# A written order for the first two blocks of an attention and expert kernel

## The chip, the cores and the metric

The kernel runs on one core of one Trainium2 chip. The time is the device time of one execution in microseconds (us), and the time of a kernel is the median of several. One further execution is recorded by the hardware profiler. The engines have names of their own in the profile: PE is TensorE (PEld its weight loads), DVE is VectorE, ACT is ScalarE, POOL is GpSimd, and SP is SyncE, which here only issues transfers. All engines run their own queues in order and wait for one another by semaphores.

## What is computed

The reference is a linear attention, followed by two matrix products with a gate between them:

```python
q_s = exp(q - max(q, axis=-1));  q_s = q_s / (sum(q_s, axis=-1) + 1e-09)
k_s = exp(k - max(k, axis=2));   k_s = k_s / (sum(k_s, axis=2) + 1e-09)
kv = einsum('bhsd,bhse->bhde', k_s, v)
x  = einsum('bhsd,bhde->bhse', q_s, kv)        # 8 batches, 8 heads, 576 rows, 64 wide
h  = x.reshape(4608, 512) @ w_in               # 512 x 2048
g  = h * clip(h + 3.0, 0.0, 6.0) / 6.0
out = g @ w_out                                # 2048 x 512
```

The weights arrive as 64-bit floats. The kernel turns them into pairs of 32-bit numbers itself, a high part and a low part, and does each of the two large products in three passes: high by high, high by low, low by high.

## The kernel before

The 4608 rows are nine blocks of 512 (`j`). The inner width of 2048 is sixteen chunks of 128 (`f`). Each chunk has its own place of 1 MB in on-chip memory, first for the raw 64-bit weights (`raw`), then for their two parts (`w_0` to `w_15`).

**Decoding a chunk** (`decode`) is a fixed chain on two engines: `Abs` of the high words into a scratch tile `v` on ACT (L148), a clamp, a shift and the sign on DVE (L149, L151, L155), the low words scaled on ACT (L158), their addition on DVE (L159), and then the split: the high part is copied by ACT (L123, or L167), the low part is `v` minus that copy. For eleven chunks the subtraction is a DVE instruction (L124). For the five chunks 6, 8, 10, 12 and 14 (`BY_DMA`) ACT also writes `v` with scale -1, rounded as the high part is, into the place of the low part (L168), and a transfer issued by GpSimd adds `v` to it (L169, `w<-v`). There are three scratch tiles `v`; one comes free when its chunk's low part is done.

**Blocks 0 and 1** do the plain three passes. `gemm1(j, f)` is twelve matmuls of 512 columns into `ph`, then ACT's `Relu` (L841), DVE's product (L842), and the split of `g` into `g_hi` (ACT) and `g_lo` (DVE). `gemm2` is twelve matmuls into the four accumulators `po`, eight with `g_hi` and four with `g_lo`. While block 0 runs, the kernel also does the attention of block 1 for four pairs of heads, decodes all chunks, and begins to make other combinations of the weights (`fast_weights`, L463 to L485, written to `wf` in device memory). From block 2 on, two chunks at a time are done with seven products of half size (`fast_pair`), whose weights come back from `wf` into a ring of places (`fetch`).

**Attention of one pair of heads** in blocks 0 and 1: maximum over the transposed `k` (DVE `km`), exponential (ACT), transposes on PE (`pe`) and copies back (ACT), softmax over `q`, transposes (`tp`) and a copy, the product `pkv` of twenty small matmuls, three short DVE steps to `kv`, the product `px`, and its split into `x_hi` (ACT) and `x_lo` (DVE). In block 0 the subtraction and the product of the `q` softmax are on POOL.

**What sets the order.** In block 0 nothing is kept in the written order: the framework's scheduler sorts the instructions of each engine by its own timing of them, with a raised priority for a few (`soon`, `store`). With block 1, PE keeps the written order (`in_order`, L958), while DVE, ACT, POOL and SP are still sorted. From block 2 on, DVE, ACT and POOL too keep the written order (L984); there the work for the next block is spread over numbered places of the loop (`plan`, `tick`, 64 to a block, filled by `half`). SP issues nearly all loads and stores and is sorted by the scheduler throughout.

Of the kernel before, what the change touches and what calls it, by code (L numbers as in the profile page):

```python
# [18 lines left out]
P = 128  # L19
# [11 lines left out]
def attention_moe(  # L31
# [102 lines left out]
    BY_DMA = range(6, 15, 2)  # L134

    def decode(f):

        n = 2 * DM
        pairs = raws.pop(f).rearrange("p (n two) -> p n two", two=2)
        low, high = pairs[:, :, 0], pairs[:, :, 1]
        v = moe.tile([P, n], F32, name="v", bufs=3)
        m = v
        nc.scalar.activation(m, high.bitcast(F32), AF.Abs)  # L148
        nc.vector.tensor_scalar(m, m, W_MIN, W_MAX, op0=ALU.max, op1=ALU.min)  # L149
        m = m.bitcast(U32)  # L150
        nc.vector.tensor_scalar(  # L151
            m, m, 3, 0x3FFFFFFF, op0=ALU.logical_shift_left, op1=ALU.bitwise_and
        )
        vu = v.bitcast(U32)
        nc.vector.scalar_tensor_tensor(  # L155
            vu, high, 0xC0000000, m, op0=ALU.bitwise_and, op1=ALU.bitwise_or
        )
        nc.scalar.activation(low, low, AF.Copy, scale=2.0**-29)  # L158
        nc.vector.tensor_tensor(vu, vu, low, op=ALU.add)  # L159
        parts = place(f, F32R, f"w_{f}").rearrange("p (s i n) -> p s i n", s=2, i=2)  # L160
        vs = v.rearrange("p (s n) -> p s n", s=2)
        if f not in BY_DMA:
            split(parts[:, :, 0], parts[:, :, 1], vs)
        else:

            hi, lo = parts[:, :, 0], parts[:, :, 1]
            nc.scalar.copy(hi, vs)  # L167
            nc.scalar.mul(lo, vs, -1.0)  # L168
            nc.gpsimd.dma_start(lo.bitcast(F32), vs, accum_op=ALU.add)  # L169
        wi[f], wo[f] = parts[:, 0], parts[:, 1]  # L170
# [35 lines left out]
    def soon(j):  # L206
        return tc.high_priority() if j in (1,) else nullcontext()

    def kv_of(j, hp, ke, vt):

        pkv = ps_a.tile([P, TB], F32, name="pkv", tag="pa")
        for c in range(NCH):
            r = slice(0, P if c < NC4 or j >= FAST else TAIL)
            for h in range(2):
                hs = slice(h * D, (h + 1) * D)
                mm(pkv[hs, 0 : D + 1], ke[r, c, hs], vt[r, c, h, :], c == 0, c == NCH - 1)
        rk = att.tile([P, 1], F32, name="rk", bufs=2)
        kv = att.tile([P, P], F32, name="kv", bufs=5)
        with soon(j):
            nc.vector.tensor_scalar_add(rk, pkv[:, D : D + 1], EPS)  # L220
            nc.vector.reciprocal(rk, rk)
            nc.vector.scalar_tensor_tensor(
                kv.rearrange("p (h d) -> p h d", h=2),
                pkv[:, 0:D].rearrange("p (o d) -> p o d", o=1).broadcast_to([P, 2, D]),
                rk,
                mask.rearrange("p (h d) -> p h d", h=2),
                op0=ALU.mult,
                op1=ALU.mult,
            )
# [12 lines left out]
    def over(t):
        return t.rearrange("p (a o) -> p a o", o=1).broadcast_to([P, n8, D])

    def q_softmax(qt, lean, pool):

        qs = qt.rearrange("p c h d -> p (c h) d")
        qm = att.tile([P, n8], F32, name="qm", bufs=2)
        qr = att.tile([P, n8], F32, name="qr", bufs=2)
        if lean:  # L250
            nc.vector.tensor_reduce(qm, qs, axis=AX.X, op=ALU.max, negate=True)
            for i in range(n8):
                nc.scalar.activation(
                    qs[:, i],
                    qs[:, i],
                    AF.Exp,
                    bias=qm[:, i : i + 1],
                    accum_out=qr[:, i : i + 1],
                )
# [5 lines left out]
        nc.vector.tensor_scalar_add(qr, qr, EPS)
        nc.vector.reciprocal(qr, qr)
        pool.tensor_mul(qs, qs, over(qr))

    def k_softmax(j, km, ke, kt):

        nc.vector.tensor_reduce(km, kt, axis=AX.X, op=ALU.max, negate=True)
# [15 lines left out]

    def both_halves(stat, op):

        swap = att.tile([P, NG], F32, name="swap", bufs=2)  # L290
        for r in range(0, P, QD):
            o = r ^ QD
            nc.gpsimd.tensor_copy(swap[r : r + QD], stat[o : o + QD])
        nc.vector.tensor_tensor(stat, stat, swap, op=op)

    def q_softmax_t(qt):

        qs = qt.rearrange("p (g d) -> p g d", d=QD)
# [10 lines left out]
        nc.vector.tensor_mul(qs, qs, across(qr))
# [735 lines left out]
```

## Time and profile before

| | us |
|---|---|
| median of 3 runs | 874.55 (874.45 to 874.63) |
| profiled execution | 874.31 |
| its span, first to last instruction | 872.5 |
| PE busy in the span | 847.6 (97%) |
| DVE busy | 622.1 (71%) |
| ACT busy | 448.7 (51%) |
| POOL busy | 81.2 (9%) |
| mean granted PE clock | 0.992 |

The profile's rows give start and length in microseconds, the engine, the line of the kernel, what is written from what, the count, and in brackets how long the engine stood idle before and for whom. Engines overlap the end of an instruction with the start of the next, so the distance from start to start is what an instruction costs in a full queue, and it is a little less than the length. The tables by stretch give busy time of each engine, with counts in brackets, then the granted PE clock (1.00 is full speed), the busy share of the transfer engines and their rate.

### The profile page before, as it was taken

Reading aid. Unit: us, or ns where it says so; the run is one execution under the profiler, and the core shown is the slowest. Engines: PE = TensorE matmul, PEld = TensorE weight load, DVE = VectorE, ACT = ScalarE, POOL = GpSimd, SP = SyncE. Lnnn points to the kernel's source line nnn. Section 1 sums busy time; section 2 is a strip of 40 time slices with the busy share of each in tenths; the row PEclk is TensorE's granted clock in tenths of the full one; section 3 lists DMA queues with packets and bytes.
Section 4 is the critical chain, followed back from the end, with each engine's and each line's share of the span. In section 5 each row is a group of like instructions: output and inputs, shape, how many; then the busy total and the mean of one; then the engine's idle time right before and its main releaser. Section 6 shows DMA issues by size and latency. Waiting matters only on the chain.

```text
span 872.5 us, 15188 instructions
## 1 busy us (share of the span) xinstructions
PE 847.6 (97%) x5380; PEld 736.7 (84%) x5380; DVE 622.1 (71%) x1271; ACT 448.7 (51%) x907; POOL 81.2 (9%) x256
## 2 busy tenths in 40 slices
PE   4799999999999999999999999999999999999998
PEld 3577777788888998989899998999898998989996
DVE  7999997787467777777776767676767766664333
ACT  7999654444344545444544444445444545454333
POOL 5000121010101010101010101010101010100000
PEclk9899999999999999999999999999999999999999
DMA  9995454538387677767786778576865676557541
GB/s 370 413 389 142 111 165 133 167 101 301 103 282 239 194 240 247 242 196 247 230 260 185 244 210 270 180 238 207 274 202 167 188 220 191 172 167 220 178 135 48
DMA packets 98203, 184.67 MB, mean 212 GB/s; under 512 B 9808, under 2 KB 24144, under 8 KB 96080
## 3 DMA queue, kind: packets, MB, share of 16 engines
q1 hardware_dynamic: 96192, 180.03, 63.9%
q0 software_dynamic: 1360, 2.62, 1.8%
q10 hardware_dynamic: 576, 1.05, 0.3%
q8 instruction: 43, 0.70, 0.3%
q14 instruction: 32, 0.26, 0.1%
HBM read 156.93 MB, written 24.12 MB: 207 GB/s over the span
## 4 chain that ended last, share of the span: by engine, by line
PE 85%; DMA 2%; ACT 2%; DVE 1%; issue 0%; ACTq 0%
PE po L91 42%; PE ph L91 33%; PE pz L91 4%; PE px L91 3%; PE pkv L91 2%; DMA w<-v 1%; DMA wf<-w 1%; ACT w L123 0%; PE pm L97 0%; ACT v L148 0%; DVE g L584 0%; DVE w L124 0%; DVE ob L874 0%; ACT w L585 0%; ACT w L168 0%
## 5 line engine op out<-in xcount | busy, mean ns | idle before, releaser
L91 PE MATMUL po<-w,w 128*128 128x512 f32 x1008 | 262.2, 394 | 0.0
L91 PEld LDWEIGHTS po<-w,w 128*128 128x128 f32 x1008 | 176.5, 189 | 28.7
L91 PE MATMUL ph<-w,w 128*128 128x256 f32 x1008 | 147.3, 282 | 0.4 <-ACT second L559 0.4
L91 PEld LDWEIGHTS ph<-w,w 128*128 128x128 f32 x1008 | 139.4, 189 | 9.7 <-ACT second L559 0.8
L91 PE MATMUL ph<-x_lo,w 128*128 128x256 f32 (+1 forms) x800 | 146.4, 304 | 0.1
L91 PE MATMUL ph<-x_hi,w 128*128 128x256 f32 (+1 forms) x592 | 138.4, 338 | 1.4 <-DVE g L842 1.2
L91 PEld LDWEIGHTS ph<-x_lo,w 128*128 128x128 f32 x800 | 114.1, 190 | 12.2 <-issue 0.4
L91 PEld LDWEIGHTS ph<-x_hi,w 128*128 128x128 f32 x592 | 97.3, 191 | 20.4 <-DVE x_lo L124 1.8
L653 POOL COPY swap<-qm 32x16 f32<-32x16 f32 x192 | 48.5, 253 | 489.3 <-DVE qm L647 483.3
L91 PE MATMUL po<-w 128*128 128x512 f32 x336 | 88.2, 395 | 0.0
L582 ACT ACTIVATE g<-second,three 128x512 f32<-128x512 f32 x56 | 40.5, 724 | 68.9 <-DVE second L580 67.7
L91 PE MATMUL po<-w,g_hi 128*128 128x512 f32 x256 | 67.9, 402 | 0.4 <-ACT g_hi L123 0.4
L91 PEld LDWEIGHTS po<-w 128*128 128x128 f32 x336 | 58.7, 188 | 10.3 <-ACT w L585 0.5
L124 DVE TENSOR_TENSOR w<-g,w 128x512 fp32r<-128x512 f32 x56 | 38.8, 693 | 32.1 <-ACT w L123 31.7
L91 PEld LDWEIGHTS po<-w,g_hi 128*128 128x128 f32 x256 | 46.7, 188 | 11.3 <-ACT g_hi L123 0.5
L584 DVE SCALAR_TENSOR_TENSOR g<-g,second 128x512 f32<-128x512 f32 x56 | 38.7, 691 | 23.0 <-ACT g L582 23.0
L539 DVE SCALAR_TENSOR_TENSOR g<-g,ph 128x256 f32<-128x256 f32 x56 | 23.5, 420 | 44.3 <-ACT g L538 44.0
L585 ACT CAST w<-g 128x512 fp32r<-128x512 f32 x56 | 34.8, 621 | 31.9 <-DVE g L584 31.9
L538 ACT ACTIVATE g<-ph,three 128x256 f32<-128x256 f32 x56 | 26.3, 470 | 45.5 <-PE ph L91 45.4
L91 PE MATMUL pz<-x_hi,w 128*128 128x256 f32 x336 | 49.1, 282 | 0.0
L586 DVE TENSOR_TENSOR w<-g,w 128x512 fp32r<-128x512 f32 x56 | 38.8, 693 | 13.8 <-ACT w L585 12.0
L539 DVE SCALAR_TENSOR_TENSOR g<-g,first 128x256 f32<-128x256 f32 x56 | 23.6, 422 | 34.8 <-ACT g L538 34.8
(158 smaller groups left out, 1219.9 us busy)
## 6 DMA issues: line engine op xcount, KB each, us to landing
w<-wf SPq DMA_DIRECT2D x392, 256.0 KB, 3.0
raw<-in_w_dram SPq DMA_DIRECT2D x16, 1024.0 KB, 13.4
out_dram<-ob SPq DMA_DIRECT2D x36, 256.0 KB, 3.3
vt<-in_v_dram SPq DMA_DIRECT2D x28, 325.0 KB, 5.1
wf<-w SPq DMA_DIRECT2D x16, 512.0 KB, 4.4
kt<-in_kT_dram SPq DMA_DIRECT2D x28, 288.0 KB, 3.1
ke<-in_k_dram SPq DMA_DIRECT2D x24, 320.0 KB, 4.1
qt<-in_qf_dram SPq DMA_DIRECT2D x28, 256.0 KB, 3.5
```

The source lines that it names most:

```text
L91: nc.tensor.matmul(out, lhsT, rhs, start=start, stop=stop, skip_group_check=goes_on)
L124: engine.tensor_sub(lo, src, hi.bitcast(F32))
L538: nc.scalar.activation(r, h, AF.Relu, bias=three, scale=1.0)
L539: nc.vector.scalar_tensor_tensor(r, r, 6.0, h, op0=ALU.min, op1=ALU.mult)
L582: nc.scalar.activation(r, second, AF.Relu, bias=three, scale=1.0)
L584: nc.vector.scalar_tensor_tensor(r, r, 6.0, second, op0=ALU.min, op1=ALU.mult)
L585: rest.append(lambda: nc.scalar.copy(two[0], r))
L586: rest.append(lambda: nc.vector.tensor_sub(two[1], r, two[0].bitcast(F32)))
L653: nc.gpsimd.tensor_copy(swaps[hp][r : r + QD], qms[hp][o : o + QD])
```

## The change

All steps of block 0, of the attention of block 1, and of the decoding are cut into small functions, one or two instructions each, and one list of names (`STEPS`) says in which order they are written. The list holds for DVE, ACT, POOL, PE and, for its length, SP. A unit `a0` to `a3` is a pair of heads of block 0 (in the order 0, 2, 1, 3), `b0` to `b3` one of block 1, `w0` to `w15` a chunk's decoding, `g0` to `g15` a chunk's `gemm1` and, as `A` and `B`, the two halves of its `gemm2`. For block 1 DVE, ACT, POOL and PE keep a written order as well, given by `tick` as in later blocks; the attention of block 2 now goes through `half`, and all of `fast_weights` is placed there too, behind block 0. `BY_DMA` keeps only chunk 7. `x_factors`, with its four GpSimd subtractions, is gone.

```diff
-    BY_DMA = range(6, 15, 2)
+    BY_DMA = (7,)
     def decode(f):
...
-        if f not in BY_DMA:
-            split(parts[:, :, 0], parts[:, :, 1], vs)
-        else:
-            hi, lo = parts[:, :, 0], parts[:, :, 1]
-            nc.scalar.copy(hi, vs)
-            nc.scalar.mul(lo, vs, -1.0)
-            nc.gpsimd.dma_start(lo.bitcast(F32), vs, accum_op=ALU.add)
+        def hi():
+            nc.scalar.copy(parts()[0], st["v"].rearrange("p (s n) -> p s n", s=2))
+        def lo():
+            hi, lo = parts()
+            vs = st["v"].rearrange("p (s n) -> p s n", s=2)
+            if f not in BY_DMA:
+                nc.vector.tensor_sub(lo, vs, hi.bitcast(F32))
+            else:
+                nc.gpsimd.dma_start(lo.bitcast(F32), vs, accum_op=ALU.add)
+        def mul():
+            vs = st["v"].rearrange("p (s n) -> p s n", s=2)
+            nc.scalar.mul(parts()[1], vs, -1.0)
...
+    STEPS = """
+        a0.k_max b0.ld_kt a0.q_max a0.q_sub a0.k_exp a1.k_max a1.k_exp a1.k_flip a1.q_max
...
+        b0.kv2 g1.B b1.k_exp w4.hi w7.load w8.load w4.lo w5.sign b1.q_max w6.mag b0.kv3
...
+    """
+    def block0(u):
+        for step in STEPS.split():
+            unit, name = step.split(".")
+            u[unit][name]()
+    def at(j, n, *fns):
+        plan.setdefault((j, n), []).extend(fns)
+    def block1():
+        for p in range(NFC // 2 - 1):
+            d = fast_weights(p)
+            for n in (0, 1, 3, 4, 5, 7):
+                at(1, 8 * (p + 1) + n, lambda d=d: next(d, None))
+        d7 = fast_weights(NFC // 2 - 1)
+        for n in (0, 1, 3, 4, 5, 8):
+            at(2, n, lambda: next(d7, None))
+        for j in range(FAST, NB):
+            lead = {FAST: 3, FAST + 1: 6}.get(j, 0)
+            half(j, 0, 2, lead)
+            half(j, 1, 3, 32, 2 if j == FAST else 0)
+        fill()
+        for f in range(NFC):
+            g = gemm1(1, f)
+            tick(1, 4 * f)
+            tick(1, 4 * f + 1)
+            g.mms()
+            g.relu()
+            tick(1, 4 * f + 2)
+            g.times()
+            g.hi()
+            if f % 2 and f >= 11:
+                fetch(2 if f < 15 else 12 - len(come))
+            keep = f == NFC - 1
+            if not keep:
+                fill(6)
+            tick(1, 4 * f + 3)
+            gs = g.lo()
+            if not keep:
+                fill(6)
+            pend.append(work(1, [f], [gs]))
+    with tc.manual_schedule(engines=ORDERED | {mybir.EngineType.SP}):
+        block0(begin())
     with tc.manual_schedule(engines=ORDERED):
+        block1()
         for j in range(FAST, NB):
```

Three places show what moves. The first is DVE in block 0, around the last splits of `x` (`x_lo0`) that the first `gemm1` needs; `v` is the scratch tile of a chunk (before, `v_326` is chunk 1, `v_358` chunk 2, `v_414` chunk 3, `v_462` chunk 4; after, `v_281` chunk 1, `v_297` chunk 2). Before:

```order
L124 TENSOR_TENSOR x_lo0_311<-px_314,x_hi0_310 128x512
L159 ISA v_358<-raw2_118,v_358 128x2048
L221 RECIPROCAL rk_293<-rk_293 128x1
L149 TENSOR_SCALAR v_414<-v_414 128x1024
L222 SCALAR_TENSOR_TENSOR kv_294<-pkv_282,rk_293,mask_86 128x128
L124 TENSOR_TENSOR w_1_333<-v_326,w_1_333 128x2x512
L151 TENSOR_SCALAR v_414<-v_414 128x1024
L124 TENSOR_TENSOR x_lo0_311<-px_318,x_hi0_310 128x512
L124 TENSOR_TENSOR w_2_365<-v_358,w_2_365 128x2x512
L155 SCALAR_TENSOR_TENSOR v_414<-raw3_120,v_414 128x1024
L149 TENSOR_SCALAR v_462<-v_462 128x1024
L124 TENSOR_TENSOR x_lo0_311<-px_322,x_hi0_310 128x512
```

And the same place of DVE in the changed kernel:

```order
L386 TENSOR_TENSOR x_lo0_314<-px_326,x_hi0_313 128x512
L161 SCALAR_TENSOR_TENSOR v_281<-raw1_118,v_281 128x1024
L161 SCALAR_TENSOR_TENSOR v_297<-raw2_120,v_297 128x1024
L171 ISA v_281<-raw1_118,v_281 128x2048
L386 TENSOR_TENSOR x_lo0_314<-px_335,x_hi0_313 128x512
L386 TENSOR_TENSOR x_lo0_314<-px_342,x_hi0_313 128x512
L273 TENSOR_REDUCE km_366<-kt_130 128x1
L171 ISA v_297<-raw2_120,v_297 128x2048
L151 TENSOR_SCALAR v_364<-v_364 128x1024
L187 TENSOR_TENSOR w_1_369<-v_281,w_1_369 128x2x512
L155 TENSOR_SCALAR v_364<-v_364 128x1024
L187 TENSOR_TENSOR w_2_375<-v_297,w_2_375 128x2x512
```

The low parts of chunks 1 and 2 stood ahead of the last `x_lo0`; they now stand behind it.

The second place is PE, where the first `gemm2` of block 0 (`po`) comes (before, `w_305`, `w_365`, `w_421` are chunks 0, 2, 3). Before:

```order
L91 MATMUL ph<-x_lo_311,w_365 128x512
L91 MATMUL ph<-x_hi_310,w_365 128x512
L91 MATMUL po<-w_305,g_hi 128x512 x8
L91 MATMUL po<-w_305,g_lo 128x512 x4
L91 MATMUL ph<-x_hi_310,w_421 128x512
L91 MATMUL ph<-x_lo_311,w_421 128x512
```

In the changed kernel (`w_289`, `w_369`, `w_418`, `w_525` are chunks 0, 1, 3, 4):

```order
L89 MATMUL ph<-x_lo_314,w_418 128x512
L89 MATMUL ph<-x_hi_313,w_418 128x512
L89 MATMUL po<-w_289,g_hi 128x512 x8
L89 MATMUL po<-w_289,g_lo 128x512 x4
L89 MATMUL po<-w_369,g_hi 128x512 x8
L89 MATMUL po<-w_369,g_lo 128x512 x4
L89 MATMUL ph<-x_hi_313,w_525 128x512
```

The first `gemm2` stood behind the `gemm1` of three chunks; it now stands behind that of four, and two chunks' `gemm2` follow each other.

The third place is SP, behind the first six raw chunks. Before:

```order
L130 DMA raw6_336<-in_w_dram 128x2048
L325 DMA kt_368<-in_kT_dram 128x576
L330 DMA vt_371<-in_v_dram 128x650
L332 DMA qt_373<-in_q_dram 128x512
L130 DMA raw7_392<-in_w_dram 128x2048
L330 DMA vt_595<-in_v_dram 128x650
L332 DMA qt_597<-in_q_dram 128x512
L130 DMA raw14_802<-in_w_dram 128x2048
L130 DMA raw12_688<-in_w_dram 128x2048
```

In the changed kernel:

```order
L259 DMA kt_130<-in_kT_dram 128x576
L264 DMA vt_292<-in_v_dram 128x650
L268 DMA qt_299<-in_q_dram 128x512
L128 DMA raw6_362<-in_w_dram 128x2048
L429 DMA wf0_1375<-w_0_289 128x2x256 x2
L429 DMA wf0_1375<-w_1_369 128x2x256
L259 DMA kt_415<-in_kT_dram 128x576
L264 DMA vt_507<-in_v_dram 128x650
L268 DMA qt_509<-in_q_dram 128x512
L128 DMA raw7_527<-in_w_dram 128x2048
```

The load of chunk 7 now stands behind stores of chunks 0 and 1 and behind the second pair of heads of block 1 (`kt_415`), whose single buffer comes free with the first pair's transposes.

More of the change, by code (lines that the diff above doesn't have):

```diff
@@ new lines, in decode, with load, raw, mag @@
+        st = {}
+        def load():
+            load_w(f)
+        def raw(which):
+            return raws[f].rearrange("p (n two) -> p n two", two=2)[:, :, which]
+        def mag():
+            st["v"] = v = moe.tile([P, n], F32, name="v", bufs=3)
+            nc.scalar.activation(v, raw(1).bitcast(F32), AF.Abs)
+        def clamp():
+            v = st["v"]
+            nc.vector.tensor_scalar(v, v, W_MIN, W_MAX, op0=ALU.max, op1=ALU.min)
+        def shift():
+            vu = st["v"].bitcast(U32)
+            nc.vector.tensor_scalar(
+                vu, vu, 3, 0x3FFFFFFF, op0=ALU.logical_shift_left, op1=ALU.bitwise_and
+            )
@@ L172, in attention_moe @@
+        return dict(
+            load=load, mag=mag, clamp=clamp, shift=shift, sign=sign, lows=lows, plus=plus, hi=hi, mul=mul, lo=lo
+        )
     FAST = 2
@@ L840, in gemm1, with mms @@
-        g = moe.tile([P, TB], F32, name="g", bufs=2)
-        nc.scalar.activation(g, ph, AF.Relu, bias=three, scale=1.0)
-        nc.vector.scalar_tensor_tensor(g, g, 6.0, ph, op0=ALU.min, op1=ALU.mult)
-        g_hi = moe.tile([P, TB], F32R, name="g_hi", bufs=3)
-        g_lo = moe.tile([P, TB], F32R, name="g_lo", bufs=3)
-        split(g_hi, g_lo, g)
-        return g_hi, g_lo
+        st = {}
+        def mms():
+            x_hi, x_lo = x_tiles[j]
+            st["ph"] = ph = ps_h.tile([P, TB], F32, name="ph", tag="ph")
+            for cc in range(NCC):
+                first, last = cc == 0, cc == NCC - 1
+                w_hi, w_lo = (wi[f][:, i, cc * P : (cc + 1) * P] for i in (0, 1))
+                mm(ph, w_hi, x_hi[:, cc, :], first, False)
+                mm(ph, w_hi, x_lo[:, cc, :], False, False)
+                mm(ph, w_lo, x_hi[:, cc, :], False, last)
@@ L848, in gemm2, with lo, A, B @@
+        def lo():
+            g_hi, g_lo = st["gs"]
+            nc.vector.tensor_sub(g_lo, st["g"], g_hi.bitcast(F32))
+            return st["gs"]
+        def A():
+            st["work"] = work(j, [f], [st["gs"]])
+            B()
+        def B():
+            for got in [next(st["work"]) for _ in range(6)]:
+                run(got)
+        return SimpleNamespace(mms=mms, relu=relu, times=times, hi=hi, lo=lo, A=A, B=B)
     def gemm2(f, g_hi, g_lo, po):
@@ L977, in attention_moe, with begin @@
[L977 to L983 removed]
+    AHEAD = 6
+    HEADS = (0, 2, 1, 3)
+    def begin():
+        nc.scalar.activation(three, three, AF.Exp)
+        nc.gpsimd.memset(three, 3.0)
+        u = {}
+        for n, hp in enumerate(HEADS):
+            load_first(hp)
+            u[f"a{n}"] = early(0, hp)
+            u[f"a{n}"]["load"]()
+            u[f"b{n}"] = early(1, hp)
+            if n == 1:
+                load_w(0)
+            if n > 1:
+                load_first_v(HEADS[n - 2])
+        for hp in HEADS[2:]:
+            load_first_v(hp)
+        for f in range(NFC):
+            if 0 < f < AHEAD:
+                load_w(f)
+            u[f"w{f}"] = decode(f)
+            u[f"g{f}"] = vars(gemm1(0, f))
+        return u
```

502 lines of the change are left out of this document (209 added, 293 removed).

## The prediction

> **What bounds the kernel now.** I read the busy times by stretch first, cut where PE's work changes: at the first large matmul (33.45 us), at a point late in the first quarter of block 0, and at the first matmul of block 1 (143.4 us).
>
> ```profile
> 0.00:33.45 33.45, 16.81 (x124) 10.80 (x124) 28.16 (x52) 27.37 (x40) 11.32 (x19) 0.90 0.96 385
> 33.45:59.08 25.63, 23.90 (x116) 18.83 (x117) 25.63 (x39) 24.17 (x57) 0.00 (x0) 0.93 1.02 415
> 59.08:143.40 84.32, 81.94 (x402) 64.32 (x401) 77.77 (x128) 58.38 (x109) 12.60 (x29) 0.98 0.55 149
> 143.40:234.50 91.10, 91.10 (x467) 73.28 (x466) 66.43 (x134) 40.56 (x75) 8.79 (x16) 1.00 0.51 170
> ```
>
> The columns are length, then PE, PEld, DVE, ACT, POOL, then PE's clock. From 143.4 us PE is busy for 91.10 of 91.10 us. Ahead of it PE misses 16.64, 1.73 and 2.38 us, and its clock is at 0.90, 0.93 and 0.98, while DVE is busy nearly throughout. So the kernel is bound by PE's work, plus what PE loses in the first 143 us. PE's matmuls are the same before and after; a change of the early order is worth what it takes from these losses. PE's own time line names them:
>
> ```profile
> 27.26 1.13 PE L91 MATMUL px<-kq,kv 128*128 128x512 f32 x2 [1.48 <-DVE x_lo L124]
> 31.21 2.04 PE L91 MATMUL px<-kq,kv 128*128 128x512 f32 x2 [2.82 <-DVE kv L222]
> 33.45 0.79 PE L91 MATMUL ph<-x_hi,w 128*128 128x512 f32 x1 [0.20 <-DVE x_lo L124]
> ...
> 47.45 1.19 PE L91 MATMUL po<-w,g_lo 128*128 128x512 f32 x4 [1.33 <-DVE g_lo L124]
> ...
> 53.15 2.13 PE L91 MATMUL po<-w,g_hi 128*128 128x512 f32 x8 [0.39 <-ACT g_hi L123]
> ...
> 82.16 0.43 PE L91 MATMUL px<-qT,kv 128*128 128x64 f32 x2 [0.69 <-ACT qT L366]
> 83.81 0.50 PE L91 MATMUL ph<-x_hi,w 128*128 128x512 f32 x1 [1.22 <-DVE g L842]
> ...
> 87.92 0.73 PE L91 MATMUL ph<-x_hi,w 128*128 128x512 f32 x2
> ...
> 108.50 0.43 PE L91 MATMUL px<-qT,kv 128*128 128x64 f32 x2 [0.47 <-ACT qT L366]
> ...
> 143.41 0.40 PE L91 MATMUL ph<-x_hi,w 128*128 128x512 f32 x1
> ```
>
> Behind 33.45 us PE stands 1.33 + 0.39 + 0.69 + 1.22 + 0.47 = 4.10 us. A stop can also halve the clock, though the one of 1.33 us at 47 us did not:
>
> ```profile
> 30.00:32.00 2.00, 0.79 (x1) 0.50 (x2) 2.00 (x5) 1.90 (x3) 0.00 (x0) 0.53 1.08 426
> ...
> 46.00:48.00 2.00, 0.67 (x3) 0.48 (x3) 2.00 (x5) 2.00 (x12) 0.00 (x0) 1.00 0.99 418
> ...
> 82.00:84.00 2.00, 0.62 (x3) 0.49 (x4) 2.00 (x4) 1.95 (x4) 0.00 (x0) 1.00 0.96 274
> 84.00:86.00 2.00, 2.00 (x7) 1.58 (x7) 2.00 (x4) 1.48 (x3) 0.00 (x0) 0.68 0.41 146
> 86.00:88.00 2.00, 2.00 (x6) 1.52 (x6) 2.00 (x5) 2.00 (x5) 0.10 (x1) 0.50 0.01 4
> ```
>
> ```profile
> 111.79 2.79 PE ph L91 x12
> ```
>
> Twelve matmuls at full clock take 2.80 us, 0.233 each (the chain of waits, above). From 83.81 to 87.92 us eleven go by in 4.11 us instead of 2.57: 1.55 us more. The first eight of `gemm1` at 33.45 us lose as much, since PE had stood for 2.82 us.
>
> **The change, term by term.** *First term: the start of `gemm1`.* It waits for the third split of `x`, which sits in DVE's queue.
>
> ```profile
> 4.39 0.75 DVE L271 TENSOR_REDUCE km<-kq 128x1 f32<-128x576 f32 x1 [4.39 <-DMA kq<-in_kT_dram]
> ...
> 18.57 3.02 POOL L267 TENSOR_TENSOR kq<-kq,qr 128x512 f32<-128x512 f32 x2 [3.86 <-DVE qr L265]
> ...
> 18.91 1.79 DVE L124 TENSOR_TENSOR w<-v,w 128x1024 fp32r<-128x1024 f32 x1
> ...
> 32.72 0.68 DVE L124 TENSOR_TENSOR x_lo<-px,x_hi 128x512 fp32r<-128x512 f32 x1
> ```
>
> What the steps in it cost:
>
> ```profile
> L155 DVE SCALAR_TENSOR_TENSOR v<-raw,v 128x1024 uint32<-128x1024 uint32 x16 | 20.1, 1257 | 0.1
> L159 DVE CUSTOM_DVE_ANT_0 v<-raw,v 128x2048 uint16<-128x2048 uint16 x16 | 19.5, 1218 | 0.1
> L124 DVE TENSOR_TENSOR w<-v,w 128x1024 fp32r<-128x1024 f32 x11 | 13.9, 1266 | 1.1 <-ACT w L123 1.0
> L149 DVE TENSOR_SCALAR v<-v 128x1024 f32<-128x1024 f32 x16 | 11.4, 713 | 1.0 <-ACT v L148 1.0
> L151 DVE TENSOR_SCALAR v<-v 128x1024 uint32<-128x1024 uint32 x16 | 11.1, 696 | 0.0
> L124 DVE TENSOR_TENSOR g_lo<-g,g_hi 128x512 fp32r<-128x512 f32 x16 | 10.9, 684 | 0.0
> ```
>
> ```profile
> 69.01 0.68 DVE L124 TENSOR_TENSOR g_lo<-g,g_hi 128x512 fp32r<-128x512 f32 x1
> 69.61 0.68 DVE L842 SCALAR_TENSOR_TENSOR g<-g,ph 128x512 f32<-128x512 f32 x1
> 70.21 1.22 DVE L159 CUSTOM_DVE_ANT_0 v<-raw,v 128x2048 uint16<-128x2048 uint16 x1
> 71.35 0.74 DVE L271 TENSOR_REDUCE km<-kt 128x1 f32<-128x576 f32 x1
> ```
>
> From start to start a 512-wide step costs 0.60 us and a 1024-wide one with two sources 1.14; clamp and shift (L149, L151) have the 512-wide step's length and cost 0.60. In the new order one clamp, one shift, one addition and one subtraction fewer stand ahead of that third split: 2 x 0.60 + 2 x 1.14 = 3.48 us. This prefix ran slower than its sum before (about 25.4 us of such costs between the first `km` at 4.39 us and 33.40 us, less 0.8 us of waiting: a factor 1.11; the subtraction at 18.91 us took 1.79 us for 1.27 while POOL worked), so I take 3.48 x 1.11 = 3.9 us: `gemm1` starts at 29.5 us. Bounds: 2 us if the rest stretches more, 5.2 if POOL's share of the stretch falls as well. That PE still starts at half clock is left in: it stands between the last `px` and the split as it does now.
>
> *Second term: the stops behind it.* The first `gemm2` now stands behind four `gemm1`s, which gives `g_lo` of chunk 0 time. By the running sum over DVE's new order, the last split of `x` ends 0.60 behind the third, at 30.1 us; chunk 1's low part has 0.66 + 1.14 + 0.60 + 1.14 ahead of its end (33.6 us), chunk 2's 0.60 + 1.14 more (35.4), chunk 3's 2 x 1.14 + 4 x 0.60 + 1.14 more (41.2), chunk 4's 7.9 more (49.1), chunk 5's 9.1 more (58.2); `g_lo` of chunk 0 is out at 41.2 + 0.60 + 1.14 + 0.60 = 43.5. PE needs 2.80 + 1.55 us for the first `gemm1`, then 2.80 per twelve matmuls, about 0.95 per `pkv`, 0.5 per set of transposes and 1.0 per `px`: it comes to chunks 1 to 5 at 34.4, 37.2, 40.9, 49.3 and 59.2 us, and to `g_lo` of chunk 0 at 45.6. So the margins are thin for chunks 3 and 4 and there is no stop of a microsecond. Behind that, each chunk costs DVE 4.62 + 1.20 us and a sixteenth of its attention, PE 5.6 and the same; DVE is the slower one per chunk, but its steps stand up to two chunks ahead.
>
> *What the four transfers cost and what replaces them.*
>
> ```profile
> w<-v POOLq DMA_DIRECT2D x5, 512.0 KB, 5.1
> ```
>
> ```profile
> ACT v L148 <- DMA w<-v: 7.0, 2, 4.9
> ```
>
> ```profile
> L168 ACT ACTIVATE w<-v 128x1024 fp32r<-128x1024 f32 x5 | 5.3, 1067 | 0.0
> ```
>
> Each transfer lands 5.1 us after its issue and keeps one of three scratch tiles until then; ACT waited 7.0 us for two of them. Four go, with four ACT copies (4.3 us) and four issues on POOL. DVE gets four subtractions, 4 x 1.14 = 4.6 us. DVE's whole share of block 0 is then 15 x 4.62 + 3.48 for decoding, 16 x 1.20 for the gate and eight heads at about 3.15, 117 us; from 4.39 us, with 0.8 us of waiting and 2.8 us of early stretch, the last `g_lo` is out at 125 us and its `gemm2` at 128. That lies ahead of PE's own end below, so the added work is hidden behind PE; if it were not, it would cost its 4.6 us.
>
> So the stops behind 33.45 us, 4.10 us, and the slow clock at 84 us, 1.55, go. I put 0.7 us for new ones, the thin margins. Bounds: none, and 5.
>
> *Third term: block 1.* It now holds all attention of block 2 and all `fast_weights`. DVE has 66.4 of 91.1 us there; the `q` softmax of three pairs and four additions that ran ahead of it come on top:
>
> ```profile
> L463 DVE TENSOR_TENSOR m<-w 128x512 f32<-128x512 f32 x4 | 2.5, 676 | 0.0
> ...
> L309 DVE TENSOR_TENSOR qt<-qt,qr 128x512 f32<-128x512 f32 x3 | 2.1, 692 | 0.1
> ```
>
> Four steps like L309 for each of three pairs are 8.3 us, the additions 2.5, small ones about 1: some 12 us, 78 of 91, 0.86. Each matmul group's `g` has the 5.6 us of another group to be ready. I take 0; bounds: -0.4 (a small stop near block 2 goes) and, as a rival, 11.
>
> The sum goes against the profiled execution, 874.31 us: 874.31 - 3.9 - 4.10 - 1.55 + 0.7 = 865.5. The median of the runs is 0.24 us above that execution, so 865.7 us. Block 1 then starts at 143.4 - 8.85 = 134.6 us. A second count agrees: at 59.1 us PE has done 24 more matmuls than now and one `px`, 6.4 us; with 0.69 + 1.22 + 1.55 + 0.47 saved later that is 10.3 us, less 1.4 for handing over between engines that the running sum leaves out.
>
> The stop at 82 us halves the clock after 1.22 us without a large matmul. [...]
>
> **The rivals.** *PE keeps its clock over the gap ahead of `gemm1` (0.05).* Then the first eight matmuls cost 1.55 us less: 864.0 to 864.2. For it: 1.00 was granted behind the stop of 1.33 us. Against: the gap will be nearer to that of 2.82 us, which cost the clock. [...]
>
> *The thin margins break (0.17).* SP's queue has the load of chunk 7 behind a store that waits for chunk 1's low part, and ACT's copies of the low words stand behind loads. If chunks 3, 4, 5 and 7 each come 1 us late, PE stands 4 us, and once or twice drops its clock (1.55 us each): 865.7 + 4 + 2 = 871.7. For it: the same engines are full (24.17 and 25.63 of 25.63 us). Against: the loads run at 415 GB/s in that stretch, and a chunk of 1 MB takes 2.5 us.
>
> *Block 1 starves, slower than before (0.13).* One mechanism: DVE at 0.86 in a fixed order waits inside its queue for POOL's swaps, PE's transposes or a load, and `g_lo` behind it comes late for each of sixteen `gemm2`s. At 0.56 us per chunk it eats the 8.85 us; at 0.8 us, with one drop of the clock, it costs 16 x 0.8 + 1.55 = 14.3: 880. For it: in a written order nothing can be pulled ahead of such a wait. Against: the same written places run in later blocks with PE full.
>
> *It doesn't do what it says (0.05):* the engines meet at the same times, because attention's chain and not the queue sets `gemm1`; only the later stops go partly: about 872.5 to 874.
>
> **How the numbers follow.** Forecast 0.60, the kept clock 0.05, the thin margins 0.17, block 1 0.13, no effect 0.05. The likeliest gives 865.7 us. Its own range is 862.2 (start at 28.2, no new stop, the half clock gone) to 869. It holds some 0.6 with the kept clock; with the thin margins up to 872 the whole range is 862.2 to 872, and what is left out is the starved block 1 and no effect. A measurement tells 0.2%, 1.75 us, from no change: faster is below 872.8. The forecast, the kept clock and most of the thin margins (0.15) are below: 0.80; same, the rest of them and no effect, 0.07; slower, the starved block 1, 0.13.
>
> **What would show it.** The first matmul of `gemm1` at 29 to 30 us; the first of block 1 near 134.6; no wait of ACT for `w<-v`; no stop of PE over 1 us between 30 and 130 us, and a clock of 1.00 there after the start; DVE's last decoding subtraction near 122 us; PE full in block 1 and at the change to block 2. The forecast is wrong if `gemm1` starts after 32 us, if PE waits for `g_lo` or `x_lo` in block 1, or if a load of a chunk ends PE's wait.

## The result, and the profile after

The changed kernel takes **867.04 us** (865.12 to 867.68), the kernel before 874.53 in the same runs: a ratio of **0.991**, 95% interval 0.9897 to 0.9923. The profiled execution took 866.55 us, 7.76 less than the one before. First the busy times by stretch (columns as before), cut where PE's work changes now, and two short stretches around the first `gemm1`:

```profile
0.00:32.02 32.02, 15.12 (x124) 10.08 (x124) 24.59 (x48) 23.19 (x36) 10.69 (x19) 1.00 0.96 381
32.02:135.51 103.49, 103.48 (x516) 82.00 (x517) 96.51 (x141) 80.72 (x161) 1.33 (x1) 0.98 0.59 203
135.51:226.00 90.49, 90.49 (x467) 73.31 (x466) 76.75 (x159) 40.05 (x71) 9.97 (x32) 1.00 0.53 169
226.00:250.00 24.00, 23.66 (x148) 20.98 (x148) 18.42 (x38) 11.38 (x23) 1.09 (x4) 1.00 0.86 288
...
32.00:34.00 2.00, 1.98 (x7) 1.64 (x8) 2.00 (x3) 1.48 (x2) 0.00 (x0) 0.81 0.22 78
34.00:36.00 2.00, 2.00 (x6) 1.41 (x5) 2.00 (x3) 1.60 (x2) 0.00 (x0) 0.50 0.00 0
```

From the first `gemm1` at 32.02 us to block 1 at 135.51 PE is busy for 103.48 of 103.49 us, and block 1 is full; at the change to block 2 it stops once, for 0.34 us. The 4.10 us of stops are gone, and so is the slow clock at 84 us (1.00 was granted from 82 to 88 us). One half clock is left, behind the gap of 2.81 us ahead of `gemm1`. PE's own time line shows that gap and the start of block 1:

```profile
32.02 0.50 PE L89 MATMUL ph<-x_hi,w 128*128 128x512 f32 x1 [2.81 <-DVE x_lo L386]
...
36.95 0.47 PE L89 MATMUL ph<-x_hi,w 128*128 128x512 f32 x1
...
135.51 0.39 PE L89 MATMUL ph<-x_hi,w 128*128 128x512 f32 x1
```

(The row at 36.95 us is the second `gemm1`.) Block 1 starts 143.41 - 135.51 = 7.90 us sooner. Of this the earlier `gemm1` is 33.45 - 32.02 = **1.43 us**, the stops 4.10, the clock at 84 us 1.55; 0.82 I cannot assign.

The start is the surprise, so here is the beginning of ACT's and DVE's time lines, first after the change (a row with q behind the engine's name issues transfers; L225 is the load of `q`):

```profile
0.75 1.28 ACT L910 ACT_TABLE_LOAD   x1 [0.75 <-PEq L1073]
1.17 0.88 ACTq L225 DMA_DIRECT2D kq<-in_q_dram  x2
...
8.54 0.69 DVE L283 TENSOR_REDUCE qm<-kq 128x8 f32<-128x512 f32 x1 [2.27 <-DMA kq<-in_q_dram]
```

and before (L198):

```profile
0.75 0.41 ACTq L198 DMA_DIRECT2D kq<-in_q_dram  x1
1.19 1.28 ACT L880 ACT_TABLE_LOAD   x1 [1.19 <-PEq L1035]
1.25 1.35 ACTq L198 DMA_DIRECT2D kq<-in_q_dram  x3
...
6.31 0.68 DVE L261 TENSOR_REDUCE qm<-kq 128x8 f32<-128x512 f32 x1
```

The new `begin` writes ACT's table load ahead of all loads, and in a written order it stays there. So the first `q` load is issued at 1.17 instead of 0.75 us, and the second row maximum, the fourth step in DVE's queue, runs at 8.54 instead of 6.31 us, with DVE idle for 2.27 us before it.

### The profile page after: what moved, and what is told of

The parts are those of the page before. It is cut to its first block, busy times and chain, and to the rows that moved or that the text cites. A ratio compares the mean times of both kernels' runs of the same rounds, so it can differ in the third digit from the quotient of the medians.

```text
span 864.5 us, 15152 instructions
## 1 busy us (share of the span) xinstructions
PE 843.4 (98%) x5380; PEld 736.5 (85%) x5380; DVE 625.2 (72%) x1275; ACT 443.3 (51%) x897; POOL 70.7 (8%) x244
## 3 DMA queue, kind: packets, MB, share of 16 engines
q10 hardware_dynamic: 576, 1.05, 0.3%
## 4 chain that ended last, share of the span: by engine, by line
PE 95%; DVE 2%; DMA 1%; ACT 1%; issue 0%; POOL 0%; ACTq 0%; POOLq 0%
PE po L89 46%; PE ph L89 39%; PE pz L89 5%; PE px L89 3%; PE pkv L89 3%; DMA kq<-in_q_dram 1%; DVE v L161 0%; PE tp L95 0%; PE pm L95 0%; PE pe L95 0%; DVE x_lo L386 0%; DVE w L187 0%; DVE v L151 0%; DVE v L171 0%; DVE qr L308 0%
## 5 line engine op out<-in xcount | busy, mean ns | idle before, releaser
L620 POOL COPY swap<-qm 32x16 f32<-32x16 f32 x224 | 58.7, 262 | 627.9 <-DVE qm L614 593.9
```

What stands on the lines that cost most here:

```text
L620: nc.gpsimd.tensor_copy(swaps[hp][r : r + QD], qms[hp][o : o + QD])
```

## The experiments

Each is the changed kernel with one edit, except where said. Ratios are to the kernel before in the same runs, where it took 874.07 to 874.58 us.

### The q loads first

```diff
-        nc.scalar.activation(three, three, AF.Exp)
-        nc.gpsimd.memset(three, 3.0)
         u = {}
         for n, hp in enumerate(HEADS):
             load_first(hp)
...
         for hp in HEADS[2:]:
             load_first_v(hp)
+        nc.scalar.activation(three, three, AF.Exp)
+        nc.gpsimd.memset(three, 3.0)
```

> The changed kernel, but the four loads of q are issued by ACT ahead of its exponential table load (and the one-element exponential that asks for it), as in the kernel before. Theory Q, gemm1 starts late because the second q load lands late: DVE's idle 2.27 us at 8.54 us shrinks to under 0.8 (it was 0.8 in the kernel before), all of DVE's queue moves up by 1.5 us or so, gemm1 starts at 30.3 to 30.7 us instead of 32.02, nothing new stops behind it since DVE's later low parts move up as well, and the time is 867.0 - 1.5 = 865.5 us (865.0 to 866.2). Rival S, the start is set by the steps themselves stretched beside GpSimd and by the handing over between engines: the idle goes, but reappears in front of a later step, gemm1 still starts at 31.6 to 32.1 us, and the time is 866.6 to 867.4.

**864.96 us** (864.53 to 865.33), ratio 0.9896 (0.9882 to 0.9909). Its time lines of ACT, DVE and PE:

```profile
0.76 1.85 ACTq L225 DMA_DIRECT2D kq<-in_q_dram  x4
...
6.49 0.68 DVE L283 TENSOR_REDUCE qm<-kq 128x8 f32<-128x512 f32 x1
...
29.96 0.49 PE L89 MATMUL ph<-x_hi,w 128*128 128x512 f32 x1 [2.82 <-DVE x_lo L386]
```

and the stretch behind the start:

```profile
30.00:59.08 29.08, 29.08 (x138) 22.95 (x139) 29.08 (x41) 25.54 (x59) 0.00 (x0) 0.94 0.80 300
```

The second maximum comes at 6.49 us without a wait, all of DVE's queue moves up, `gemm1` starts 2.06 us sooner than in the changed kernel, and PE is full behind it. Theory Q, with a little more gained than it said. Since the intervals of the two kernels touched, both ran again side by side:

> The changed kernel, unchanged, beside the next one on one chip, since the two were so far timed apart (867.04 and 864.96 us with overlapping intervals). Theory Q (the late second q load): DVE's idle in front of the second q maximum is 2 to 3.5 us in the profile and the median 866.5 to 867.7. Rival R (the two differ by the chip and the day alone): the median is within 1 us of the next kernel's.

> The changed kernel with the four q loads ahead of ACT's table load, a second time, beside the changed kernel. Theory Q: gemm1 starts near 30 us, 864.5 to 865.7, 1.5 to 2.5 us below the changed kernel with an interval that excludes none. Rival R: within 1 us of it.

The changed kernel took 866.96 us (865.50 to 867.71), with the `q` loads first 864.64 (864.47 to 864.85): 2.3 us apart, and no run of the one within the range of the other. Their profiles, the changed kernel's rows of DVE and PE first:

```profile
9.02 0.69 DVE L283 TENSOR_REDUCE qm<-kq 128x8 f32<-128x512 f32 x1 [2.83 <-DMA kq<-in_q_dram]
...
32.50 0.71 PE L89 MATMUL ph<-x_hi,w 128*128 128x512 f32 x1 [2.81 <-DVE x_lo L386]
```

```profile
30.00 0.50 PE L89 MATMUL ph<-x_hi,w 128*128 128x512 f32 x1 [2.82 <-DVE x_lo L386]
```

`gemm1` starts 2.50 us apart. Why 0.4 us at the issue become 2 us and more at the landing is not shown. What the rows have is this: in the profiles of the kernel before, the changed kernel and the first one with the `q` loads first SP issues the 1 MB load of chunk 0 at 1.66 or 1.67 us, about when the second `q` load is issued in the changed kernel, and the transfer engines are full from about 4 us on (1.09 of their time from 4 to 6 us in the changed kernel). That load was not moved.

### x before the decoding

On DVE the last splits of `x` are put ahead of part of chunk 1's and 2's decoding; the work up to chunk 1's low part stays the same.

```diff
-        a1.x_mm a1.x_hi a1.x_lo a3.q_flip a2.x_mm w1.lows w1.sign w2.sign w1.plus a3.q_copy
-        a3.x_mm a2.x_hi a2.x_lo w4.lows a3.x_hi a3.x_lo g0.mms w6.load w3.mag b0.k_max
+        a1.x_mm a1.x_hi a1.x_lo a3.q_flip a2.x_mm a3.q_copy a3.x_mm a2.x_hi a2.x_lo w1.lows
+        w1.sign a3.x_hi a3.x_lo g0.mms w1.plus w2.sign w4.lows w6.load w3.mag b0.k_max
```

> The changed kernel, but on DVE the splits of x stand ahead of the sign and addition of chunk 1 and the sign of chunk 2, so that only the first gemm1 gets its operands sooner, while the sum of DVE's work up to chunk 1's low part is the same. Theory D, DVE's queue sets the pace of the first 60 us as a whole: gemm1 starts near 29.5 us, but PE then waits about 2 us for the low part of chunk 1, which still ends near 36.1 us, and the second gemm1 ends no sooner; the time is 866.5 to 868 (the added stop may cost the clock). Rival G, the start of gemm1 is what counts, as the prediction's first term has it: the time falls by about 2.5 us, to 864.5.

869.08 us (867.54 to 870.54), ratio 0.9944 (0.9931 to 0.9957): slower than the change as it is. PE's time line:

```profile
29.04 0.50 PE L89 MATMUL ph<-x_hi,w 128*128 128x512 f32 x1
...
36.59 1.33 PE L95 MATMUL pe<-ident,kt 128*128 128x128 f32 x5 [4.49 <-ACT kt L276]
37.57 0.78 PE L89 MATMUL ph<-x_hi,w 128*128 128x512 f32 x1
```

and a stretch behind it, for the clock:

```profile
38.00:40.00 2.00, 2.00 (x6) 1.52 (x6) 2.00 (x4) 1.32 (x2) 0.00 (x0) 0.50 0.60 153
```

`gemm1` starts 3 us sooner and runs at full clock, and all of it is lost one step later: PE stands 4.49 us, not for the low part of chunk 1 as I had expected but for the transposes of block 1's first `k`. Their exponential on ACT stands behind chunk 2's high part, which waits 0.80 us for DVE. The second `gemm1` starts at 37.57 us (36.95 in the changed kernel), and at half clock. So theory D in its substance, with a median 1.1 us above its range: an earlier start is worth something only where DVE's whole queue comes earlier, as with the `q` loads.

### PE kept at work ahead of gemm1

With the `q` loads first, sixteen transposes of the identity stand on PE ahead of `gemm1`.

```diff
+        def warm():
+            t = ps_o.tile([P, TB], F32, name="warm", tag="po")
+            for c in range(16):
+                flip(t[:, c % 4 * P : (c % 4 + 1) * P], ident)
...
-        a3.x_mm a2.x_hi a2.x_lo w4.lows a3.x_hi a3.x_lo g0.mms w6.load w3.mag b0.k_max
+        a3.x_mm a2.x_hi a2.x_lo w4.lows a3.x_hi a3.x_lo k.warm g0.mms w6.load w3.mag b0.k_max
```

> The changed kernel with the q loads ahead of the table load (864.96 us) and, on PE, sixteen transposes of the identity into a free accumulator tile behind the last px, so that PE is at work for some 2 of the 2.82 us for which it stands ahead of gemm1. They compute nothing that is used. Theory C, the clock falls to 0.50 because PE stands: the first gemm1 then runs at full clock, 2.80 us instead of about 4.3, and as DVE's low part of chunk 1 ends near 34.0 us, PE waits for it about 0.5 to 1 us; the time is 864.0 to 864.7. Rival K, the slow clock has another cause, since the other stops of 1.2 to 2.3 us ahead of it did not lower it: 0.50 is granted for some 3 us all the same, 864.7 to 865.4.

865.63 us (864.81 to 865.87), ratio 0.9894 (0.9878 to 0.9911): no gain over the `q` loads alone. But the clock held, as one stretch of this kernel shows (the mean granted clock of its four runs was 0.999 to 1.000, that of the eight runs with the `q` loads alone 0.997 to 0.999):

```profile
32.00:34.00 2.00, 2.00 (x10) 1.50 (x8) 2.00 (x3) 1.10 (x2) 0.00 (x0) 1.00 0.27 97
```

and its PE time line shows what the clock was worth:

```profile
28.31 1.91 PE L95 MATMUL warm<-ident 128*128 128x128 f32 x16
31.21 0.51 PE L89 MATMUL ph<-x_hi,w 128*128 128x512 f32 x1 [1.00 <-DVE x_lo L386]
...
35.36 0.76 PE L95 MATMUL pe<-ident,kt 128*128 128x128 f32 x5 [1.08 <-ACT kt L276]
35.88 0.48 PE L89 MATMUL ph<-x_hi,w 128*128 128x512 f32 x1
```

The first `gemm1` is through about 3.1 us after its start, and PE then waits 1.08 us for the transposes of block 1's first `k`. From the first to the second `gemm1` are 35.88 - 31.21 = 4.67 us; in the changed kernel, where the clock falls some 1.2 us behind the start (an estimate from the 0.81 granted between 32 and 34 us and the 0.50 behind it), 36.95 - 32.02 = 4.93. So the half clock costs 0.26 us there, not the 1.55 that the prediction put on its matmuls: DVE's and ACT's chain to those transposes takes the rest. Where it fell earlier it cost more. The kernel with four transfers back, told of below, is the same up to here, and its clock was 0.50 from 32 to 38 us; its PE time line:

```profile
32.98 0.80 PE L89 MATMUL ph<-x_hi,w 128*128 128x512 f32 x1 [2.81 <-DVE x_lo L386]
...
38.80 0.48 PE L89 MATMUL ph<-x_hi,w 128*128 128x512 f32 x1
```

That is 5.82 us, 1.15 more than at full clock.

Theory C holds for the clock and fails for the time, which lies above both expectations. In this profile `gemm1` started 1.25 us later than with the `q` loads alone: some 8 us ahead of the added transposes DVE had waited 1.48 us for a `pkv`. That is more than the kept clock can give back here.

A kept clock is seen without any transposes too, in the kernel with sixteen repeats, told of below, which is the changed kernel's code up to block 1. Its profile has the gap of 2.82 us, and the clock stayed. PE's time line and a stretch:

```profile
32.88 0.50 PE L89 MATMUL ph<-x_hi,w 128*128 128x512 f32 x1 [2.82 <-DVE x_lo L386]
...
37.55 0.48 PE L89 MATMUL ph<-x_hi,w 128*128 128x512 f32 x1
```

```profile
34.00:36.00 2.00, 1.95 (x9) 1.24 (x7) 2.00 (x4) 1.12 (x2) 0.00 (x0) 1.00 0.00 0
```

Again 37.55 - 32.88 = 4.67 us. So a gap of 2.81 or 2.82 us in this place halved the clock (to 0.50) in seven profiles, the changed kernel's and those with the `q` loads first among them, and left it at 1.00 in this one. What decides between the two is not shown.

### gemm2 one place earlier on PE

```diff
-        w4.sign g0.lo b0.kv1 g3.mms w6.lows w4.plus b1.k_max g1.hi g1.lo w5.clamp b0.q_exp0
-        b0.q_exp1 b0.q_over1 w5.shift g2.relu g2.times g0.A g0.B b1.ld_vt b1.ld_qt g1.A
+        w4.sign g0.lo b0.kv1 w6.lows w4.plus b1.k_max g1.hi g1.lo w5.clamp b0.q_exp0
+        b0.q_exp1 b0.q_over1 w5.shift g2.relu g2.times g0.A g0.B g3.mms b1.ld_vt b1.ld_qt g1.A
```

> The changed kernel, but on PE alone the first gemm2 stands ahead of the fourth gemm1, one gemm1 sooner; all other engines keep their order. In the changed kernel the fourth gemm1 starts at 43.60 and chunk 0's g_lo is out at 46.0 us. Theory P, the prediction's second term, the new place of that gemm2 on PE is what takes away the stop for g_lo: its four matmuls with g_lo would be reached at 43.6 + 8 x 0.233 = 45.5 us, PE stops about 0.5 us, and the fourth gemm1 with its g comes 2.8 us later, so that DVE, which has chunk 3's product in a fixed place, waits too: 867.5 to 870. Rival O, the order on DVE is what matters and PE has slack in where its groups stand: no stop above 0.6 us, 866.7 to 867.4.

867.99 us (866.18 to 868.72), ratio 0.9929 (0.9916 to 0.9943). PE's time line:

```profile
32.50 0.50 PE L89 MATMUL ph<-x_hi,w 128*128 128x512 f32 x1 [2.82 <-DVE x_lo L386]
...
43.20 0.95 PE L89 MATMUL pkv<-vt,ke 128*64 128x65 f32 x20
...
46.50 1.19 PE L89 MATMUL po<-w,g_lo 128*128 128x512 f32 x4 [0.28 <-DVE g_lo L831]
```

and the same operand in the changed kernel, first on DVE, then on PE:

```profile
45.30 0.68 DVE L831 TENSOR_TENSOR g_lo<-g,g_hi 128x512 fp32r<-128x512 f32 x1
```

```profile
48.38 1.10 PE L89 MATMUL po<-w,g_lo 128*128 128x512 f32 x4
```

A stop of 0.28 us, no other up to block 2, and a time that the runs do not tell from the changed kernel's, though it lies in theory P's range. The stop is as small as rival O said, and chunk 3's later product holds nothing up; but O's reason, the order on DVE, does not fit the rows. PE waited for this `g_lo` until 46.50 - 32.50 = 14.00 us behind the start of `gemm1`, and in the kernel before until 47.45 - 33.45 = 14.00 us as well. In the changed kernel DVE has it done at 45.98 us, 13.96 behind that start. So against the start of `gemm1` DVE's new order brings `g_lo` no sooner. What differs is when PE comes to it: 12.67 us behind the start before, 13.72 here, 16.36 in the changed kernel. Most of the first difference is the product `pkv` at 43.20 us, which in the kernel before comes behind this `gemm2`, at 51.81 us; the second is the fourth `gemm1`. So by these rows PE's order takes this stop away: about 0.9 of the 1.33 us by the earlier `pkv`, the last 0.28 by the place of `gemm2`; some 0.15 I cannot assign.

### The transfers, in three orders

Four transfers back in the written order:

```diff
-    BY_DMA = (7,)
+    BY_DMA = range(6, 15, 2)
...
-        w6.hi w6.lo b1.q_mul g5.hi w8.mag w8.clamp g5.lo w8.shift b1.kv_mm b1.kv1 w8.sign
+        w6.hi w6.mul w6.lo b1.q_mul g5.hi w8.mag w8.clamp g5.lo w8.shift b1.kv_mm b1.kv1 w8.sign
```

and so for chunks 8, 10, 12 and 14, with `w7.mul` taken out.

> The changed kernel with its written order, but chunks 6, 8, 10, 12 and 14 make their low part by the copy with scale -1 on ACT and the adding transfer, and chunk 7 on DVE. DVE has four subtractions of 1.14 us less, ACT four copies of about 1.07 us more, and each transfer keeps one of three scratch tiles 5.1 us. Theory T, the transfers are what cost the kernel before its later stops: ACT, in a fixed order, waits for scratch tiles again (7.0 us in all before), PE stops for g_hi or g_lo behind that, 2 to 5 us, and the time is 869 to 872. Rival H, the transfers were hidden, and the written order alone gives the gain: no stop of PE behind 32 us, the time within 1 us of 867.0.

**896.83 us** (895.35 to 897.38), ratio 1.0258 (1.0244 to 1.0272): slower than both kernels by over 20 us. PE's waits (us in total, times, longest):

```profile
PE ph L89 <- DMA w<-v: 20.9, 5, 9.8
```

the time lines of SP, POOL and PE at the longest of them:

```profile
67.73 0.42 SPq L128 DMA_DIRECT2D raw<-in_w_dram  x1
...
68.68 0.43 SPq L128 DMA_DIRECT2D raw<-in_w_dram  x1
...
69.86 0.45 SPq L128 DMA_DIRECT2D raw<-in_w_dram  x1
...
70.45 1.33 POOL L189 DMA_DIRECT2D w<-v  x1 [45.39 <-ACT w L193]
...
82.85 0.79 PE L89 MATMUL ph<-x_hi,w 128*128 128x512 f32 x1 [9.78 <-DMA w<-v]
```

and a stretch inside it:

```profile
76.00:80.00 4.00, 0.00 (x0) 0.00 (x0) 0.64 (x1) 0.00 (x0) 0.00 (x0) 0.50 1.05 280
```

The list puts `gemm1` of a chunk right behind its low part, which suits a DVE step of 1.2 us. PE had begun chunk 6 and stood inside it 9.78 us for the transfer, and with PE in a fixed order ACT and DVE soon stood too. PE's wait for the transfer ended some 12 us after its issue. SP had issued three chunk loads of 1 MB within the 3 us before it, and the transfer engines were at 1.05; that these loads delayed it is not tested. The time moves the way theory T said, by 29.8 us where it had 2 to 5, and by another wait: not ACT's for scratch tiles (1.7 us) but PE's own, for the low part. This does not tell what a list made for five transfers would take.

The same code sorted by the framework's scheduler in block 0, with one transfer and with five (both have the moved work of block 2 and block 1's written order):

```diff
     def ordered(ins):
-        tc.keep_in_program_order(ins)
+        if in_order:
+            tc.keep_in_program_order(ins)
...
-    with tc.manual_schedule(engines=ORDERED | {mybir.EngineType.SP}):
-        block0(begin())
+    block0(begin())
+    in_order.append(True)
```

> The changed kernel without the written order of block 0: all engines are sorted by the framework's scheduler there, as in the kernel before; one transfer, the small steps and block 1's written order stay. Theory O, the written order carries the gain: gemm1 starts near 33 us or later, PE has stops of over 1 us between 33 and 135 us again, and the time is 872 to 877. Rival W, what carries it is the work moved behind block 0 and the transfers that left: 866 to 869 with PE full from 32 us on.

> The changed kernel without block 0's written order (870.17 us with one transfer), and with five transfers (chunks 6, 8, 10, 12, 14) instead of chunk 7's. Theory P, a transfer costs only where gemm1 of its chunk has a fixed place close behind it: a sorted order steps around it as in the kernel before, PE waits for w<-v at most 1 us in all, and the time is 868 to 873. Rival X, the transfers themselves are too slow for this block whatever the order: 885 to 900 as in the written order.

And the kernel before with `BY_DMA = (7,)` as its only edit:

> The kernel before, its order sorted by the framework's scheduler as ever, but with one adding transfer (chunk 7) in place of five: the transfers' share of the change alone. Theory T, the transfers caused the later stops of the kernel before (ACT waited 7.0 us for their scratch tiles): the stops at 82 to 84 us and the slow clock there go (0.69 + 1.22 + 1.55 us), 871 us. Rival H, in a sorted order they cost nothing since other work is pulled ahead, and DVE's 4.6 us more are hidden or not: 873.5 to 876.

| block 0 | five transfers, us | one, us |
|---|---|---|
| sorted, block 2's work partly in block 0 (the kernel before) | 874.5 | 879.04 (877.91 to 879.73) |
| sorted, block 2's work behind block 0 | 874.46 (874.21 to 876.05) | 870.17 (869.65 to 870.71) |
| written order (the change: one transfer) | 896.83 | 867.04 |

The edit to one transfer costs 4.5 us in the first row, gains 4.3 in the second and nearly 30 in the third. In the first, with one transfer, PE's largest stop behind its start is for DVE's product `g`, and block 1 isn't full; PE's time line, and two stretches:

```profile
91.55 0.50 PE L91 MATMUL ph<-x_hi,w 128*128 128x512 f32 x1 [3.73 <-DVE g L842]
```

```profile
59.08:143.40 84.32, 80.59 (x399) 63.82 (x398) 77.24 (x124) 54.21 (x103) 9.56 (x21) 0.98 0.39 119
143.40:234.50 91.10, 89.31 (x450) 71.02 (x449) 69.46 (x142) 41.20 (x76) 9.48 (x20) 0.98 0.54 176
```

Its time lies above both of its expectations. The four subtractions are 4.6 us of DVE's time, and the loss is of that size; that they are its cause is only argued, since with this edit the scheduler also sorts block 0 anew (DVE's order differs from 60 us on). In the second, with one transfer, PE is all but full behind 59 us although block 0's order is not written; the time lies between the two expectations, and `gemm1` starts at 30.14 us, not near 33. Its PE time line at the start, and two stretches:

```profile
35.32 0.80 PE L92 MATMUL ph<-x_lo,w 128*128 128x512 f32 x1 [2.29 <-DVE x_lo L389]
```

```profile
59.08:143.40 84.32, 84.08 (x417) 65.70 (x418) 69.52 (x103) 54.93 (x103) 1.33 (x1) 1.00 0.40 120
143.40:234.50 91.10, 90.76 (x475) 73.65 (x474) 79.46 (x164) 40.86 (x73) 9.79 (x32) 1.00 0.54 175
```

With five transfers there, ACT waits for scratch tiles again, as its waits show:

```profile
ACT v L150 <- DMA w<-v: 4.9, 2, 2.8
```

With one, DVE has 69.52 us of work between 59.08 and 143.40 us instead of 77.77 in the kernel before, and 79.46 instead of 66.43 in block 1. With five transfers the time lies 1.5 us above theory P's range, while PE has no wait for `w<-v`.

Moving block 2's work behind block 0 (with the smaller parts of the change, and block 1 in a written order) gives 879.04 - 870.17 = 8.9 us with one transfer and nothing with five (874.46 against 874.58 in the same runs). The removal of four transfers alone loses 4.5. So the two pay only together, some 4.4 us. Block 0's written order gives the last 3.1, near the start, where the sorted kernel still stands 2.29 us inside its first `gemm1`. In that sorted kernel the `q` loads land 6.2 us after their issue (median of four), near the 6.1 of the kernel before and not the 7.4 of the changed kernel; against the written order with the `q` loads first (864.64 us) the order is worth 5.5.

### DVE loaded further in block 1

```diff
             gs = g.lo()
+            g.lo()
```

> The changed kernel, but in block 1 DVE does each of the sixteen subtractions for g_lo twice, the second time the same into the same tile: 16 x 0.60 = 9.6 us more for DVE, 77.0 + 9.6 = 86.6 of 91 us. Theory L, DVE has room there as long as its sum stays under PE's: PE stays full from 135 to 226 us, 866.5 to 867.7. Rival V, the starving block of the prediction is near, and at 0.95 waits inside DVE's queue show at once: PE stops for g_lo by 0.3 to 0.6 us in most of the sixteen chunks, 872 to 878.

The same behind `if f % 2:`, in eight chunks:

> The changed kernel, but in block 1 DVE does the subtraction for g_lo twice in the eight odd chunks only: 8 x 0.60 = 4.8 us more for DVE, 77.0 + 4.8 = 81.8 of 91 us (0.90). Theory B, room in DVE's queue counts by the stretch and most of it is gone already: stops of PE by about half of what sixteen repeats brought (7.3 us), 869.5 to 871.5. Rival L, there is room for this much: 866.5 to 868.

| DVE's added work, us | time, us |
|---|---|
| 0 | 867.04 |
| 4.8 | 868.70 (867.60 to 869.24) |
| 9.6 | 874.33 (873.29 to 875.92) |

Block 1 with sixteen repeats as one stretch, then PE's time line there:

```profile
135.00:226.00 91.00, 87.15 (x443) 68.33 (x442) 80.60 (x162) 35.70 (x63) 10.55 (x32) 1.00 0.47 152
```

```profile
176.13 0.33 PE L89 MATMUL px<-qT_lo,kv_hi 128*128 128x128 f32 x1 [1.21 <-DVE qT_lo L650]
199.28 0.29 PE L95 MATMUL pm<-ident,km 128*128 128x128 f32 x1 [1.06 <-DVE km L593]
```

and with eight, the same stretch:

```profile
135.00:226.00 91.00, 90.49 (x465) 72.65 (x464) 80.21 (x164) 38.73 (x69) 10.44 (x32) 1.00 0.52 168
```

With eight the time lies between the two expectations, and its range just meets that of the changed kernel in the same runs (866.96 us, 865.50 to 867.71); PE loses 0.51 us in the stretch. With sixteen it is rival V, and the whole gain of the change is gone. PE's longer stops are not at `g_lo` but at block 2's attention, whose steps stand in the same DVE queue. Counted as 77 us plus the added work, DVE was still free enough at 77 of 91 us; at 82 it is at the edge; at 87 PE stands. (The busy time measured in the window is 80.21 and 80.60 us; with sixteen repeats block 1 runs on beyond 226 us.)

## Why the prediction was right, and where it was off

**The time:** 867.04 us for a forecast of 865.7, within its range. The mechanism was the one predicted; one term of the sum was too large. That the forecast came within 1.3 us although this term missed by 2.5 is partly luck, as the other errors went the other way.

**First term, mis-sized: the start of `gemm1`.** Predicted 29.5 us, a gain of 3.9; measured 32.02, a gain of 1.43, below the term's own lower bound of 2. The forecast's own test "wrong if `gemm1` starts after 32 us" was met by a hair, and more clearly in five other profiles of code that is the same up to there (32.15 to 32.98 us). The failing step is the one that counted instructions ahead of the third split and took all else in that queue as unchanged. The loads were not: the table load now stands ahead of the `q` loads, and DVE waits 2.27 us. The rows for it were there: the order of the new `begin` on ACT's queue, and the loads' place in the kernel before. With the `q` loads first `gemm1` starts at 29.96 and 30.00 us, 3.45 to 3.49 sooner than before, for a counted 3.48; the factor of 1.11 on it is not borne out.

**Second term, right and a little too cautious.** No stop between 32.02 and 226 us, where 0.7 us of new ones were put in. The thin margins at chunks 3 and 4 held, and with the `q` loads first too, where PE and DVE both run 2 us sooner (29.08 of 29.08 us). The reason given holds for the first stop: against the start of `gemm1` the running sums put `g_lo` of chunk 0 at 43.5 - 29.5 = 14.0 us and PE at 45.6 - 29.5 = 16.1, and 13.96 and 16.36 were measured. For the later stops no run separates the order from the work that left block 0; in the sorted kernel with one transfer those behind 59 us are nearly gone as well (84.08 of 84.32 us).

**The transfers.** That their subtractions are hidden holds in the changed kernel, where PE is full; in the kernel before the same edit lost 4.5 us, close to the bound of 4.6, though there the order changed too. DVE's last decoding subtraction starts at 124.03 us, for 122 said. I had not seen how much the written order depends on their absence.

**Third term, right.** DVE was put at 78 of 91 us in block 1 and has 76.98 of 91.00 between 135 and 226 us, with PE full. The rival that block 1 starves was near: 9.6 us more of DVE's work bring it about, at 874.3.

**The start of block 1:** 134.6 us predicted, 135.51 measured. The term for the start gave 2.5 less; the stops that did not come gave 0.7 and the unassigned part 0.8 back. **The kept clock**, a rival at 864.0 to 864.2, did not come: the half clock behind the gap was granted as forecast. But its price was put too high, since what follows the first `gemm1` waits for DVE and ACT: 0.26 us in the changed kernel and 1.15 where the clock was half from the start, where 1.55 was said.

The version with the `q` loads ahead of the table load beats both kernels: 864.64 us, ratio 0.9887 (0.9873 to 0.9900).

## What to carry to other kernels

When an order is written out by hand, write the first loads ahead of everything, since nothing will pull them past a step that merely stands first (here the table load, for 2.3 us of the time). Where two engines run close, look for the queue that sets the pace as a whole: starting one consumer sooner gains nothing if the next operand comes no sooner (here `gemm1` 3 us sooner, and 869.08 us for 867.04). To see what took a stop away, count both sides from a common start: the operand's end and the time at which its reader comes to it. Price an offload in the order that it will run in: the same four transfers were worth 4.5 us in the kernel before, cost 4.3 once work had been moved off DVE, and cost 30 in a written order that has the reader close behind.

## What was not expected of the hardware

- An adding transfer of 512 KB landed 5.1 us after its issue in the kernel before (median of five). Issued behind three 1 MB loads, with the transfer engines at 1.05, one landed 12.4 us after its issue.
- A load issued about 0.4 us later delayed its reader by 2.2 us (6.31 to 8.54 us), and by 2.7 in a second profile.
- A gap of PE of 2.81 or 2.82 us ahead of the same code halved the clock (to 0.50) in seven profiles and left it at 1.00 in one. With 1.91 us of transposes inside it, it stayed at 1.00 in one profile as well.
